# Separate readiness for three copies of V, a later gate broadcast, a one-bank gate through DRAM and new scheduler constants, in a two-branch attention kernel

## The chip, the cores and the metric

One core of a Trainium2 chip. The metric is device time in microseconds (us) of one execution. A kernel is run several times on a chip, alternating with the kernel before, and its median is given. A profiled execution gives a span from first to last instruction, some 2 us shorter than the measured time; spans are compared only with spans, times only with times.

Engines: PE is the matrix engine (PEld its weight loads), ACT the scalar engine, DVE the vector engine, POOL the GpSimd engine, SP the engine that issues most transfers.

## The reference, cut to what matters

```python
g = sigmoid((x * gate_w).sum(-1, keepdims=True))
a = softmax_attention(x, A_wqkv, A_wo)     # 2048 tokens, width 512, 32 heads of 16
b = linear_attention(x, B_wqkv, B_wo)      # phi = elu + 1
return g * a + (1 - g) * b
```

The softmax of `a` needs 32 x 2048 x 2048 exponentials. Cut into tiles of 128 keys by 512 queries that is 2048 score tiles, and they are nearly all of the kernel's work.

## The kernel before: the parts that matter

The kernel is built by a list scheduler written in the kernel itself. It holds tasks as generators, keeps a model of when each engine and each buffer is free, and each time emits the candidate that can start first. Some thirty constants steer its choices. The order on each engine is fixed when the program is built.

Score tiles leave PE in PSUM. Two thirds of them are read by ACT in pairs (one exponential of 128x1024 into a ring `P` of ten buffers), one third by DVE with an integer trick into `Z`. A `Z` tile stands for three terms, shifted by POOL or DVE; each term is multiplied in P.V with its own scaled copy of V. The three copies of a block of V are made so (the cast by DVE, two scalings by POOL):

```python
def t_v(t8, vb):
    ...                                   # V projection of one block into a bank
    yield dv(607, lambda: nc.vector.tensor_copy(Vc[:, 0, vs, :, :, 0:16], src), [r_bank[b]], [r_V[vs]])
    yield ("FREE", b)
    for k in range(1, NTERM):             # NTERM = 3
        yield po(690, lambda k=k: nc.gpsimd.tensor_scalar(... Vc[:, k, vs] <- Vc[:, 0, vs] * COEF[k] ...), [r_V[vs]], [r_V[vs]])
    yield ("FLAG", lambda: V_ready.add((t8, vb)))
...
def cand_pv():
    ...
    if (t8, w["kb"] // 4) not in V_ready:
        continue
```

One resource `r_V[vs]` and one flag stand for all three copies: a P.V that reads the plain copy waits for both scalings. The gate's logits come from 64 matmuls into four banks, after a broadcast of the gate weights on POOL:

```python
def t_gate():
    yield po(900, lambda: nc.gpsimd.tensor_copy(gwr, gwc... .to_broadcast([128, NCC, 128])), [r_gw], [r_gwr])
    ...
    for qc in range(NQC):                 # four banks, 16 matmuls of 32x512 each
        ...
        yield dv(607, lambda b=b: nc.vector.transpose(gl, bank(b)), ...)
        yield po(250, ...)
    yield ac(300, lambda: nc.scalar.activation(gt[:], ge[:], ACT.Exp, scale=-1.0), ...)
    ...
add_task(t_gate(), 0, 1, "GATE")
```

The softmax here doesn't subtract the row's maximum and nothing guards it: scores larger than these inputs give would overflow.

## Time and profile before

The time before is 675.63 us (median of 3 runs, 675.01 to 676.53). What matters of its profile (span 674.2 us):

| part of ACT's time | us |
|---|---|
| start to the first exponential | 9.31 |
| holes between exponentials up to 46 us (0.21, 2.48, 0.34, 0.17) | 3.20 |
| 695 exponentials of a pair of tiles, 0.917 each | 637.3 |
| other work of ACT between them (the rest) | 16.7 |
| last exponential ends at | 666.49 |
| drain from there to the end | 7.7 |

A hole is idle time of ACT; the drain is what follows the last exponential. From 46 us on ACT is idle only once more before its last exponential, for 0.11 us at 530.6. Most of the lines that carry this are in the prediction below. First, POOL's own timeline of the kernel before, around the largest hole (start, length, what, count, idle before it and what ended that):

```profile
22.38 0.61 POOL L1001 COPY T<-gwc 128x512 bf16<-128x512 bf16 x1 [1.23 <-DMA gwc<-in_gate_w_dram]
23.07 1.47 POOL L995 TENSOR_SCALAR Vc<-Vc 128x576 bf16<-128x576 bf16 x2
26.71 1.43 POOL L995 TENSOR_SCALAR Vc<-Vc 128x576 bf16<-128x576 bf16 x2 [2.17 <-DVE Vc L992]
```

The gate broadcast stands in POOL's queue ahead of the V scalings and waits 1.23 us for a transfer. Second, PE's instructions from the end of the last exponential to the end of the program (line, what, count, busy us, mean ns):

```profile
L383 PE MATMUL ps<-wA,OAT 128*32 128x512 bf16 x43 | 3.7, 381 | 0.1
L383 PE MATMUL ps<-wA,xnat 128*32 128x512 bf16 x32 | 2.7, 380 | 0.0
```

The drain is mainly 75 matmuls of the output projection that the scheduler had not placed earlier.

### The profile page before, as it was taken

To read this page: it belongs to the slowest core of one execution; us is meant where nothing else is said; L and a number is where in the kernel's file an instruction comes from. 1 tells how busy PE (TensorE), PEld (TensorE's weight loads), DVE (VectorE), ACT (ScalarE), POOL (GpSimd) and SP (SyncE) were. 2 spreads that over 40 slices of the span, in tenths; PEclk is the share of its full clock that TensorE was granted. 3 is DMA by queue.
4 is the path that set the end of the run, shared out by engine and by line. 5 is a ranking of instruction groups with operands and counts; after the bars stand their busy time and mean duration, and the time that the engine had idled before them with its cause. 6 is when DMAs were issued, how large, how long until landed. Compare 5 with 4: busy or idle time off the path is not lost.

```text
span 674.2 us, 23975 instructions
## 1 busy us (share of the span) xinstructions
PE 660.7 (98%) x9813; PEld 202.2 (30%) x9839; DVE 603.4 (89%) x1053; ACT 658.3 (98%) x735; POOL 559.4 (83%) x617
## 2 busy tenths in 40 slices
PE   8999999999999999999999999999999999999998
PEld 3322323232322232323333322232232332222222
DVE  6999989988888889989999888999899998899985
ACT  6899999999999999999999999999999999999996
POOL 3789888888978888888888888878888989887881
PEclk9999999999999999999999999999999999999999
DMA  6420001200000000000001000001010020000001
GB/s 133 135 84 11 6 1 36 70 10 2 3 10 1 10 2 3 10 2 11 4 2 45 30 10 1 8 12 30 6 34 10 18 42 25 24 19 11 26 17 33
DMA packets 28155, 15.96 MB, mean 24 GB/s; under 512 B 19984, under 2 KB 27024, under 8 KB 28048
## 3 DMA queue, kind: packets, MB, share of 16 engines
q1 hardware_dynamic: 26704, 13.92, 8.2%
q8 instruction: 79, 1.29, 0.8%
q10 hardware_dynamic: 1344, 0.52, 0.3%
q14 instruction: 28, 0.23, 0.1%
HBM read 6.69 MB, written 2.10 MB: 13 GB/s over the span
## 4 chain that ended last, share of the span: by engine, by line
PE 50%; ACT 31%; issue 12%; SPq 2%; DVE 2%; POOL 1%; DMA 1%; ACTq 0%; DVEq 0%; POOLq 0%
PE ps L377 39%; ACT P L778 30%; PE ps L383 10%; SPq L354 2%; DVE Z L692 1%; ACT eb L1083 1%; POOL Z L746 1%; DMA gwc<-in_gate_w_dram 1%; DVE Z L756 0%; POOL Vc L995 0%; SPq L358 0%; ACTq L1495 0%; DVE OAT L1059 0%; DVE wA L1176 0%; DVE T L1031 0%
## 5 line engine op out<-in xcount | busy, mean ns | idle before, releaser
L778 ACT ACTIVATE P<-ps 128x1024 bf16<-128x1024 f32 x695 | 645.5, 1117 | 3.9 <-PE ps L377 3.7
L746 POOL TENSOR_TENSOR Z<-Z,mcon 128x512 int32<-128x512 int32 x471 | 488.0, 1061 | 64.4 <-DVE Z L692 50.4
L692 DVE TENSOR_SCALAR Z<-ps 128x512 int16<-128x512 f32 x658 | 440.4, 683 | 57.2 <-PE ps L377 50.9
L377 PE MATMUL ps<-Qz,KT 32*128 32x512 bf16 x2048 | 271.8, 384 | 3.9 <-ACT P L778 1.7
L377 PE MATMUL ps<-Z,Vc 128*17 128x512 bf16 x1974 | 272.5, 382 | 0.5 <-DVE Z L756 0.3
L377 PE MATMUL ps<-P,Vc 128*17 128x512 bf16 x1390 | 245.0, 383 | 1.0 <-POOL Vc L995 1.0
L377 PEld LDWEIGHTS ps<-Qz,KT 32*128 32x128 bf16 x2048 | 67.8, 91 | 262.7 <-ACT P L778 228.7
L377 PEld LDWEIGHTS ps<-Z,Vc 128*17 128x17 bf16 x1974 | 60.9, 88 | 69.1 <-issue 44.2
L756 DVE TENSOR_SCALAR Z<-Z 128x1024 int16<-128x1024 int16 x187 | 77.3, 433 | 0.0
L377 PEld LDWEIGHTS ps<-P,Vc 128*17 128x17 bf16 x1390 | 55.5, 88 | 60.1 <-issue 46.0
L377 PE MATMUL ps<-warm 128*32 128x512 bf16 (+16 forms) x529 | 55.9, 326 | 4.7 <-issue 2.4
L383 PE MATMUL ps<-xT,wA 128*32 128x512 bf16 (+1 forms) x528 | 43.4, 376 | 0.0
L1084 POOL TENSOR_SCALAR eb<-eb 128x512 f32<-128x512 f32 x32 | 21.0, 656 | 18.7 <-DVE Z L756 10.1
L995 POOL TENSOR_SCALAR Vc<-Vc 128x576 bf16<-128x576 bf16 x32 | 21.7, 679 | 6.0 <-DVE Vc L992 2.3
L377 PEld LDWEIGHTS ps<-warm 128*32 128x32 bf16 (+1 forms) x555 | 19.4, 96 | 18.4 <-issue 10.3
L383 PE MATMUL ps<-wA,OAT 128*32 128x512 bf16 x256 | 23.0, 382 | 0.1
L1071 POOL TENSOR_TENSOR T<-T,rg 128x256 bf16<-128x256 f32 x31 | 19.6, 631 | 4.1 <-PE ps L377 1.0
L1083 ACT ACTIVATE eb<-ps 128x512 f32<-128x512 f32 x32 | 22.7, 709 | 0.0
L383 PE MATMUL ps<-xT,wB 128*32 128x512 bf16 x256 | 22.3, 382 | 0.0
L383 PE MATMUL ps<-wA,xnat 128*32 128x512 bf16 x256 | 22.3, 381 | 0.0
L1035 DVE STREAM_TRANSPOSE T<-ps 128x512 f32<-128x512 f32 x31 | 21.9, 706 | 0.1
L1085 DVE SCALAR_TENSOR_TENSOR phiK<-ps,eb 128x512 bf16<-128x512 f32 x32 | 21.7, 678 | 0.2 <-POOL eb L1084 0.2
(81 smaller groups left out, 276.1 us busy)
## 6 DMA issues: line engine op xcount, KB each, us to landing
Qz<-QT SPq DMA_DIRECT2D x120, 16.0 KB, 1.8
wA<-in_A_wqkv_dram SPq DMA_DIRECT2D x4, 384.0 KB, 4.3
wB<-in_B_wqkv_dram SPq DMA_DIRECT2D x4, 384.0 KB, 3.0
xnat<-in_A_x_dram SPq DMA_DIRECT2D x3, 512.0 KB, 3.8
out_dram<-outt SPq DMA_DIRECT2D x12, 128.0 KB, 1.7
wA<-in_A_wo_dram SPq DMA_DIRECT2D x1, 512.0 KB, 4.6
wA<-in_B_wo_dram SPq DMA_DIRECT2D x1, 512.0 KB, 6.5
out_dram<-wA SPq DMA_DIRECT2D x4, 128.0 KB, 1.7
```

Source lines behind the costliest of these rows:

```text
L377: return lambda: nc.tensor.matmul(o, lhsT=l, rhs=r, start=start, stop=stop, skip_group_check=sg)
L383: h = nc.tensor.matmul(o[32 * j:32 * j + 32], lhsT=l[:, 32 * j:32 * j + 32], rhs=r, start=start, stop=stop, skip_group_check=True)
L692: return C(DV, OPP, 533 * n + 74, lambda: nc.vector.tensor_scalar(o, i, ZB, 0.0, op0=ALU.add, op1=ALU.max), [r_bank[b] for b in bks], r_Z[ ...
L746: return C(PO, 400, 70 + 484 * n, lambda: nc.gpsimd.tensor_tensor(Z[:, z, 0:512 * n].bitcast(I32), Z[:, z0, 0:512 * n].bitcast(I32), mcon[ ...
L756: return C(DV, 450 if hot else 300, 69 + 134 * n, lambda: nc.vector.tensor_scalar(Z[:, z, 0:512 * n], Z[:, z0, 0:512 * n], float(m), None, ...
L778: return C(AC, 500, 427 * n + 49, lambda: nc.scalar.activation(P[:, slot, 0:512 * n], bank(b0, n), ACT.Exp, scale=ESC), [r_bank[b0 + k] fo ...
L995: yield po(690, lambda k=k: nc.gpsimd.tensor_scalar(Vc[:, k, vs].rearrange("p a b c -> p (a b c)"), Vc[:, 0, vs].rearrange("p a b c -> p ( ...
L1035: yield dv(607, lambda: nc.vector.transpose(T1[:, a, :], bank(7)), [r_bank[7]], [r_T1[a]])
L1071: yield po(640, lambda k=k: nc.gpsimd.tensor_tensor(dst_[:, k], src[:, k, :, 0:16], rgc[:, k].unsqueeze(2).to_broadcast([128, 16, 16]), AL ...
L1083: yield ac(480, lambda: nc.scalar.activation(eb[:, i, :], bank(b), ACT.Exp), [r_bank[b]], [r_eb[i]])
L1084: yield po(640, lambda: nc.gpsimd.tensor_scalar(eb[:, i, :], eb[:, i, :], 1.0 + 1e-6, 0.0, op0=ALU.min, op1=ALU.max), [r_eb[i]], [r_eb[i]])
L1085: yield dv(607, lambda: nc.vector.scalar_tensor_tensor(dst_ap, bank(b), 1e-6, eb[:, i, :], op0=ALU.max, op1=ALU.add), [r_bank[b], r_eb[i]] ...
```

## The change

Its intent: let P.V start on the plain copy of V as soon as that one is cast; keep the gate out of the way in the ramp; make the gate cheaper on PE, DVE and POOL, at the price of a trip through a small DRAM buffer; and search the scheduler's constants anew. The core of the diff:

```diff
-    HOT = 32.85
-    BACK = 980.186
-    SHB = 2
+    HOT = 31.272
+    BACK = 977.283
+    SHB = 3
 ... (thirteen more constants: PMIN, PLATE, SLK, DSL, AGE, PEP, HOLD, NACT, BIAS, TTOL, MTR, PQS, KR)
-        DMIN = 4
+        DMIN = 3
-        r_V = [R(f"V{p}") for p in range(NVQ)]
+        r_V = [[R(f"V{p}_{k}") for k in range(NTERM)] for p in range(NVQ)]
 ...
-        dma(SP, gwc[:], gate_w..., semG, 16, 3000.0, ...)
+        dma(SP, gwc[:], gate_w..., semG, 16, 6000.0, ...)
 ...
-                    if (t8, w["kb"] // 4) not in V_ready:
+                    if (t8, w["kb"] // 4, w["term"]) not in V_ready:
 ...
-                for x in (w["res"], r_V[vs]):
+                for x in (w["res"], r_V[vs][w["term"]]):
 ...
-            yield dv(607, ... [r_bank[b]], [r_V[vs]])
+            yield dv(607, ... [r_bank[b]], [r_V[vs][0]])
+            yield ("FLAG", lambda: V_ready.add((t8, vb, 0)))
 ...
-                                   ... [r_V[vs]], [r_V[vs]])
-            yield ("FLAG", lambda: V_ready.add((t8, vb)))
+                                   ... [r_V[vs][0]], [r_V[vs][k]])
+                yield ("FLAG", lambda k=k: V_ready.add((t8, vb, k)))
 
         def t_gate():
-            yield po(900, ... to_broadcast([128, NCC, 128])), [r_gw], [r_gwr])
+            yield po(400, ... to_broadcast([128, NCC, 32])), [r_gw], [r_gwr])
 ...          # one bank: 16 matmuls, four column groups side by side; one transpose
+            yield ac(230, ... ge[:, 0, :] <- exp(-logits, 128x16) ...)
 ...
+            yield ("DMA", scr, ge[:, 0, :], semGN, 16, ...)                     # rows to DRAM
+            for a in range(4):
+                yield ("DMA", gt[32 * a:32 * (a + 1), :, :], scr..., semGT, 64, ...)   # and back, spread
 ...
-        add_task(t_gate(), 0, 1, "GATE")
+        add_task(t_gate(), 0.5, 1.2, "GATE")
```

The number 6000.0 in the load of the gate weights is only the scheduler's belief of when that load lands; it makes the broadcast look ready later, and so it is emitted later.

More of the change, by code (lines that the diff above doesn't have):

```diff
@@ L159, in bass_gated_mix__mha_block__linear_attn_block__prompt_kernel @@
     FILL = 0.7
-    HOT = 32.85
-    BACK = 980.186
-    SHB = 2
+    HOT = 31.272
+    BACK = 977.283
+    SHB = 3
     why = [None]
-    PMIN = 2
-    PLATE = -199.667
-    SLK = 88.975
-    DSL = 843.776
+    PMIN = 1
+    PLATE = -168.321
+    SLK = 188.531
+    DSL = 812.862
     STICK = 65.578
@@ L171, in bass_gated_mix__mha_block__linear_attn_block__prompt_kernel @@
     DENS = 0.743
-    AGE = 300.0
-    PEP = 148.771
+    AGE = 140.993
+    PEP = 147.128
     PVD = 216
@@ L176, in bass_gated_mix__mha_block__linear_attn_block__prompt_kernel @@
     MZD = 0.0
-    HOLD = 109.508
-    NACT = 4
-    BIAS = 82.599
+    HOLD = 16.447
+    NACT = 5
+    BIAS = 65.881
     KEYW = 7.061
@@ L182, in bass_gated_mix__mha_block__linear_attn_block__prompt_kernel @@
     DTOL = 186.116
-    TTOL = 37.928
-    PKR, MTR, PQR, PQS, FR = 0.404, 8.73, 13.55, 1.600, 0.0
-    KR, KS, QR = 5.59, 1.48, 4.00
+    TTOL = 64.585
+    PKR, MTR, PQR, PQS, FR = 0.404, 8.00, 13.55, 1.667, 0.0
+    KR, KS, QR = 6.12, 1.48, 4.00
     NB = 2
@@ L231, in bass_gated_mix__mha_block__linear_attn_block__prompt_kernel @@
         T2 = SB([128, 2, 512], BF16, "T2")
-        gwr = T2[:, 0, :].rearrange("p (c n) -> p c n", c=NCC)
+        gwr = T2[:, 0, 0:128].rearrange("p (c n) -> p c n", c=NCC)
         OAT = SB([128, NT8, S], BF16, "OAT")
@@ L242, in bass_gated_mix__mha_block__linear_attn_block__prompt_kernel @@
         gt = SB([128, NQC, 16], FP32, "gt")
-        ge = SB([128, NQC, 16], FP32, "ge")
+        ge = SB([128, 2, 16], FP32, "ge")
+        gp = SB([128, 4, 16], FP32, "gp")
+        scr = nc.dram_tensor("gate_rows", [128, 16], FP32).ap()
         gnat = SB([128, NKB], FP32, "gnat")
@@ L288, in bass_gated_mix__mha_block__linear_attn_block__prompt_kernel @@
         r_mcon = R("mcon")
-        r_gt, r_ge, r_gl, r_gnat = R("gt"), R("ge"), R("gl"), R("gnat")
+        r_gt, r_ge, r_gl, r_gp, r_gnat, r_scr = R("gt"), R("ge"), R("gl"), R("gp"), R("gnat"), R("scr")
         r_OBT = [R(f"OBT{i}") for i in range(NKB)]
@@ L399, in bass_gated_mix__mha_block__linear_attn_block__prompt_kernel @@
         semGN = SEM("s_gn")
+        semGP = SEM("s_gp")
+        semGT = SEM("s_gt")
         semOB = [SEM(f"s_ob{i}") for i in range(2)]
@@ L418, in bass_gated_mix__mha_block__linear_attn_block__prompt_kernel @@
                 r_xT[t][h].tw = SP.free + 2900.0
-        dma(SP, gwc[:], gate_w.rearrange("(cc p) -> p cc", p=128), semG, 16, 3000.0, writes=[r_gw], noncontig=True, issue=500.0)
+        dma(SP, gwc[:], gate_w.rearrange("(cc p) -> p cc", p=128), semG, 16, 6000.0, writes=[r_gw], noncontig=True, issue=500.0)
         emit(DV, 200, lambda: nc.vector.memset(warm[:], 0.0), writes=[r_warm])
@@ L436, in bass_gated_mix__mha_block__linear_attn_block__prompt_kernel @@
         for p in range(NVQ):
-            emit(PO, 200, lambda p=p: nc.gpsimd.memset(Vc[:, 0, p].rearrange("p t h d -> p (t h) d")[:, :, 16:18], 1.0), writes=[r_V[p]])
+            emit(PO, 200, lambda p=p: nc.gpsimd.memset(Vc[:, 0, p].rearrange("p t h d -> p (t h) d")[:, :, 16:18], 1.0), writes=[r_V[p][0]])
         for k, m in enumerate(SHIFTS[1:]):
@@ L991, in t_v @@
             src = bank(b).rearrange("p (t h d) -> p t h d", t=4, h=8)
-            yield dv(607, lambda: nc.vector.tensor_copy(Vc[:, 0, vs, :, :, 0:16], src), [r_bank[b]], [r_V[vs]])
+            yield dv(607, lambda: nc.vector.tensor_copy(Vc[:, 0, vs, :, :, 0:16], src), [r_bank[b]], [r_V[vs][0]])
+            yield ("FLAG", lambda: V_ready.add((t8, vb, 0)))
             yield ("FREE", b)
@@ L996, in t_v @@
                                                                   Vc[:, 0, vs].rearrange("p a b c -> p (a b c)"), COEF[k], 1.0,
-                                                                  op0=ALU.mult, op1=ALU.mult), [r_V[vs]], [r_V[vs]])
-            yield ("FLAG", lambda: V_ready.add((t8, vb)))
+                                                                  op0=ALU.mult, op1=ALU.mult), [r_V[vs][0]], [r_V[vs][k]])
+                yield ("FLAG", lambda k=k: V_ready.add((t8, vb, k)))
@@ L1000, in t_gate @@
         def t_gate():
-            yield po(900, lambda: nc.gpsimd.tensor_copy(gwr, gwc[:].unsqueeze(2).to_broadcast([128, NCC, 128])), [r_gw], [r_gwr])
-            yield ("WAIT", lambda: ("x", 0) in flags and phi_free[0])
-            phi_free[0] = False
-            for qc in range(NQC):
-                b = yield ("BANK",)
-                for h in range(2):
-                    yield pe_step(2, 512, [mmt(bank(b), gwr[:, cc, :], xT[:, cc, 512 * qc:512 * (qc + 1)], start=(cc == 0), stop=(cc == NCC - 1))
-                                           for cc in (2 * h, 2 * h + 1)], [r_xT[qc][h], r_gwr], [r_bank[b]])
-                yield dv(607, lambda b=b: nc.vector.transpose(gl, bank(b)), [r_bank[b]], [r_gl, *r_outt])
-                yield ("FREE", b)
-                yield po(250, lambda qc=qc: nc.gpsimd.tensor_copy(ge[:, qc, :], gl.rearrange("p (a b) -> p a b", b=32)[:, :, 0]),
-                         [r_gl, *r_outt], [r_ge])
@@ L1013, in t_gate @@
-            phi_free[0] = True
-            yield ac(300, lambda: nc.scalar.activation(gt[:], ge[:], ACT.Exp, scale=-1.0), [r_ge], [r_gt])
-            yield po(200, lambda: nc.gpsimd.tensor_scalar(ge[:], gt[:], 1.0, None, op0=ALU.add), [r_gt], [r_ge])
-            yield dv(650, lambda: nc.vector.reciprocal(gt[:], ge[:]), [r_ge], [r_gt])
-            gp = ge[:].rearrange("p q c -> p (q c)")
-            yield po(200, lambda: nc.gpsimd.tensor_scalar(gp.rearrange("p (a u) -> p a u", a=4), gt[:].rearrange("p q (c a) -> p a (q c)", a=4),
-                                                          -1.0, 1.0, op0=ALU.mult, op1=ALU.add), [r_gt], [r_ge])
@@ L1020, in t_gate, with g4, go @@
-            for a in range(4):
-                yield ("DMA", gnat[32 * a:32 * (a + 1), :], gp[32 * a:32 * (a + 1), 16 * a:16 * (a + 1)], semGN, 64, 2500.0, [r_ge], [r_gnat], False, a == 0)
+            yield po(400, lambda: nc.gpsimd.tensor_copy(gwr, gwc[:].unsqueeze(2).to_broadcast([128, NCC, 32])), [r_gw], [r_gwr])
+            yield ("WAIT", lambda: all(("x", t) in flags for t in range(NQC)))
+            b = yield ("BANK",)
+            def g4(cc):
+                def go():
+                    for j in range(4):
+                        h = nc.tensor.matmul(bank(b)[32 * j:32 * j + 32], lhsT=gwr[:, cc, :], rhs=xT[:, cc, 512 * j:512 * (j + 1)],
+                                             start=(cc == 0), stop=(cc == NCC - 1), skip_group_check=True)
+                    return h
+                return go
@@ new lines, in t_gate @@
+            for h in range(2):
+                yield pe_step(2, 512, [g4(2 * h), g4(2 * h + 1)], [*[r_xT[t][h] for t in range(NQC)], r_gwr], [r_bank[b]])
+            yield dv(607, lambda: nc.vector.transpose(gl, bank(b)), [r_bank[b]], [r_gl, *r_outt])
+            yield ("FREE", b)
+            yield ac(230, lambda: nc.scalar.activation(ge[:, 0, :], gl.rearrange("p (a b) -> p a b", b=32)[:, :, 0], ACT.Exp, scale=-1.0),
+                     [r_gl, *r_outt], [r_ge])
+            yield po(150, lambda: nc.gpsimd.tensor_scalar(ge[:, 1, :], ge[:, 0, :], 1.0, None, op0=ALU.add), [r_ge], [r_ge])
@@ new lines, in t_gate @@
+            yield dv(170, lambda: nc.vector.reciprocal(ge[:, 0, :], ge[:, 1, :]), [r_ge], [r_ge])
+            yield ("DMA", scr, ge[:, 0, :], semGN, 16, 2500.0, [r_ge], [r_scr], False, True)
+            for a in range(4):
+                yield ("DMA", gt[32 * a:32 * (a + 1), :, :], scr.rearrange("(q i) b -> i q b", q=NQC), semGT, 64, 2800.0, [r_scr], [r_gt], False, a == 0)
+            yield po(200, lambda: nc.gpsimd.tensor_scalar(gp[:], gt[:].rearrange("p q (c a) -> p a (q c)", a=4), -1.0, 1.0, op0=ALU.mult, op1=ALU.add),
+                     [r_gt], [r_gp])
@@ L1022, in t_gate @@
+            for a in range(4):
+                yield ("DMA", gnat[32 * a:32 * (a + 1), :], gp[32 * a:32 * (a + 1), a, :], semGP, 64, 2500.0, [r_gp], [r_gnat], False, a == 0)
             yield ("FLAG", lambda: flags.add("gate"))
@@ L1101, in t_wo @@
         def t_wo():
-            yield ("WAIT", lambda: all((NT8 - 1, t) in K_ready and (NT8 - 1, t) in V_ready for t in range(NQC)))
+            yield ("WAIT", lambda: all((NT8 - 1, t) in K_ready and (NT8 - 1, t, NTERM - 1) in V_ready for t in range(NQC)))
             yield ("DMA", woA, A_wo.rearrange("(i p) n -> p i n", p=128), semWO, 32, 5000.0, [], [r_wAk], False, True)
```

## The prediction

> **What bounds the kernel now.** I read the page's part 1, then the table of stretches, then the timeline of each engine where ACT has holes. The attention has 4 x 16 x 32 = 2048 score tiles of 128x512. ACT takes 1390 of them (695 exponentials of two tiles each), DVE takes the other 658 with a bit trick (into Z), which POOL and DVE then shift twice each. All of them feed P.V on PE. Page and stretches (columns of a stretch: length, busy us and instructions of PE, PEld, DVE, ACT, POOL, then PE clock, DMA share, GB/s):
>
> ```profile
> PE 660.7 (98%) x9813; PEld 202.2 (30%) x9839; DVE 603.4 (89%) x1053; ACT 658.3 (98%) x735; POOL 559.4 (83%) x617
> ...
> 0.00:20.00 20.00, 18.05 (x268) 7.74 (x269) 14.28 (x26) 13.56 (x16) 9.44 (x32) 1.00 0.61 126
> 20.00:40.00 20.00, 18.86 (x377) 6.89 (x375) 17.97 (x31) 16.71 (x19) 16.02 (x20) 1.00 0.41 124
> 40.00:60.00 20.00, 20.00 (x264) 5.39 (x260) 18.91 (x35) 20.00 (x24) 16.62 (x22) 1.00 0.17 52
> 320.00:360.00 40.00, 39.77 (x816) 14.21 (x804) 36.98 (x67) 40.00 (x45) 34.32 (x37) 1.00 0.01 3
> ```
>
> From 40 us on ACT is busy in every microsecond until its last exponential; PE's 98% includes 529 warm-up matmuls that can give way. So the body is ACT's queue of work, and time can be won only before 40 us, after the last exponential, or by giving ACT less. ACT's own timeline (start, length, what, count, idle before it):
>
> ```profile
> 9.31 12.02 ACT L778 ACTIVATE P<-ps 128x1024 bf16<-128x1024 f32 x13 [0.54 <-PE ps L377]
> 21.54 1.02 ACT L778 ACTIVATE P<-ps 128x1024 bf16<-128x1024 f32 x1 [0.21 <-PE ps L377]
> 25.05 9.46 ACT L778 ACTIVATE P<-ps 128x1024 bf16<-128x1024 f32 x10 [2.48 <-PE ps L377]
> 34.85 2.86 ACT L778 ACTIVATE P<-ps 128x1024 bf16<-128x1024 f32 x3 [0.34 <-PE ps L377]
> 37.88 7.44 ACT L778 ACTIVATE P<-ps 128x1024 bf16<-128x1024 f32 x8 [0.17 <-PE ps L377]
> ...
> 201.59 158.87 ACT L778 ACTIVATE P<-ps 128x1024 bf16<-128x1024 f32 x173
> ...
> 649.79 16.70 ACT L778 ACTIVATE P<-ps 128x1024 bf16<-128x1024 f32 x18
> ```
>
> One exponential costs (158.87 - 1.11) / 172 = 0.917 us of ACT (1.11 is the group's mean length; neighbours overlap). After the ramp's first there are holes of 0.21 + 2.48 + 0.34 + 0.17 = 3.20 us. The last exponential ends at 649.79 + 16.70 = 666.49, and the drain to 674.2 is 7.7 us. What holds the 2.48 us open is seen in DVE, POOL and PE there, and in the chain of waits (its pieces: start, length, what):
>
> ```profile
> 18.28 4.05 DMA gwc<-in_gate_w_dram
> 22.33 0.05 issue
> 22.38 0.61 POOL T L1001
> ...
> 20.77 0.68 DVE L992 CAST Vc<-ps 128x512 bf16<-128x512 f32 x1
> ...
> 23.07 1.47 POOL L995 TENSOR_SCALAR Vc<-Vc 128x576 bf16<-128x576 bf16 x2
> ...
> 22.72 0.39 PE L377 MATMUL ps<-Qz,KT 32*128 32x512 bf16 x2
> 23.27 0.35 PE L377 MATMUL ps<-warm 128*128 128x448 bf16 x1 [0.16 <-issue]
> 24.60 0.40 PE L377 MATMUL ps<-P,Vc 128*17 128x512 bf16 x4 [0.98 <-POOL Vc L995]
> ```
>
> V's second block is cast by 21.45. POOL could scale its two copies at once, but its queue holds the gate broadcast first, and that waits for the gate weights, the last small load behind a serial run of transposing loads. The copies end at 24.54; P.V waits for both although it reads the unscaled one; the ten P buffers are full, so the fifteenth exponential waits for the P.V that frees the fifth buffer, 24.60 + 0.40 = 25.00.
>
> **The Trainium skill.** "Trainium Architecture — The Big Picture", section "Inside one NeuronCore", says that each engine has its own instruction stream and meets the others only through semaphores. The trace agrees: an idle POOL instruction (1.23 us of waiting) delays PE and ACT by queue order. "ScalarE: Activation LUTs", section "What ACT_TABLE_LOAD costs", gives 186 ns + 0.833 ns per element, with 93 ns overlapped; so halving the 1024 elements saves 427 ns. The trace has 0.917 us per exponential against an estimate of 0.946 by that formula, and the 512-wide exponential eb at 56.26 is followed at 56.73, 0.47 us later: the difference, 0.45, agrees. "TensorEngine Tiling (Array Packing)", section "Available Configurations", lists four tiles of 128x32; the trace agrees, 16 such projection matmuls take 1.05 us at 21.74, some 0.21 per wave of four after the first. "DMA: Bandwidth & Descriptors", section "Two DMAs through the same engine are not ordered", asks for the semaphore between a write and a dependent read; the changed program waits so between the gate rows' write and their reads, a full landing more. Small ones took 1.7 (gnat) to 4.0 us (gwc).
>
> **The change, part by part.** The order of the changed program was built, not run.
> 1. Own readiness per V copy. In the changed order PE runs the same two score matmuls at about 22.7, then at once the P.V of the unscaled second block, with no wait on POOL. So it starts at 22.7 + 0.32 = 23.0 instead of 24.60, ends about 23.4, and the fifteenth exponential starts at 23.4 instead of 25.05. The one before has a single P.V wave ahead of it instead of two, 0.21 less, so the hole of 0.21 goes. The hole left is 23.4 - (21.33 + 1.02) = 1.05. Sum here: (0.21 + 2.48) - 1.05 = **1.64 us** won.
> 2. Gate broadcast later. POOL now does two shifts, the second block's copies and another shift first (20.0 + 2 x 1.06 + 1.5 + 1.06, estimate 24.6), when the gate weights (22.33) have long landed: POOL's 1.23 us of waiting goes. But PE no longer waits there, so it adds nothing to part 1.
> 3. One bank of gate logits. 64 matmuls of 32x512 become 16: 12 waves x 0.21 = 2.5 us of PE, three transposes x 0.71 = 2.1 us of DVE, about 0.8 + 0.4 of POOL (four copies x 0.20 go, a 128-column broadcast instead of 512), and on ACT the 128x64 exponential (its neighbours start 0.14 apart) becomes 128x16, saving under 0.1. All but ACT's part lies beside ACT's queue. Before 40 us freed PE time may shorten the 0.34 and 0.17 holes; by hand I find one P.V-bound hole of about 0.25 at the gate matmuls, so **0.2 us** for the pair.
> 4. The trip through DRAM. One write and four reads before the gate can be used. My estimate: logits ready near 34, write issued near 38 behind eight Qz copies, landed 40, reads issued over 2.4 us (four gnat issues took 2.41) and landed near 45. The first reader is POOL near 47, and the first use of the gate is at 58.6 today. Hidden, with 2 us to spare on POOL: **0**.
> 5. Retuned scheduler constants. DVE takes 659 tiles, ACT 694 pairs and one single: 0.917 - 0.47 = **0.45 us** less on ACT. POOL gets 473 shifts instead of 471 (+2.1 us) and DVE one tile more (0.68), on engines with 83 and 89%: free. In the drain the last wait on DVE is followed by 8 output matmuls instead of 12, **0.2 us**.
> Sum: 1.64 + 0.2 + 0.05 + 0.45 + 0.2 = 2.5 us off 675.63 gives 673.1.
>
> **Rivals.** (a) *The hole is hidden anyway*: if ACT were paced by PE or DVE later, a ramp gain would be eaten by a later wait. For it: PE is 98% busy, DVE 89%. Against: no hole on ACT after 38 us; then 675. (b) *The DRAM trip becomes the new wait*: POOL stands in order behind the read of gt; if the landing takes 4 us each as gwc did, twice, POOL would stall 2 to 3 us, shifts come late, and PE's P.V with them. The ten P buffers hide most; it would give back 1 to 2 us: 674 to 675. (c) *The retuned schedule removes more*: 0.917 us per exponential may hold small waits that never show as idle because neighbours overlap; if the new constants remove a fifth of a possible 10 us, 671. (d) *ACT's new bound in the ramp is the P ring once more*: the 1.05 stays or grows if V's third and fourth blocks come late; then 674.
>
> **Range and chances.** The centre is 673.1; (b) and (d) pull up by one or two, (c) down by two; runs differ by 0.75 around the median. 80%: 671.4 to 674.9. Two per cent is 13.5 us, more than all holes and the drain's spare together (3.7 + part of 7.7), so faster is very unlikely. Slower by 13.5 would take a schedule that starves ACT, and the instruction order shows the same interleave: 1%.
>
> **What would show it.** In the changed profile: the P.V by the second V block starts near 23.0 with no wait on POOL's copies; the hole on ACT near 22.4 is about 1 us; the broadcast on POOL is 128 wide, after the second block's copies, and waits for nothing; the last exponential ends near 664.2, ahead of 666.49; drain near 7.5; no wait on the gate's reads over 1 us. The prediction is wrong if ACT shows new holes after 40 us, if the cadence in the long row moves off 0.917 by more than 0.004 (2.8 us over 694), or if the drain grows.

## The result

The changed kernel took 674.41 us (674.00 to 674.79, 4 runs) beside 675.77 us of the kernel before on the same chip (675.01 to 676.53, 4 runs). The ratio is 0.998, with a 95% interval of 0.9962 to 0.9997. (A ratio here and below is the mean of one kernel's runs over the mean of the other's of the same rounds, so not quite the ratio of the medians.) That is within 2%, 1.4 us lower, and inside the predicted range; the profiled span went from 674.2 to 672.6. A second set of runs gave 673.79 beside 676.01 (ratio 0.9964), 2.2 us lower. The prediction's sum was 2.5.

ACT's timeline of the changed kernel, from the first exponential on:

```profile
9.11 13.17 ACT L782 ACTIVATE P<-ps 128x1024 bf16<-128x1024 f32 x14 [0.53 <-PE ps L379]
23.25 4.69 ACT L782 ACTIVATE P<-ps 128x1024 bf16<-128x1024 f32 x5 [0.97 <-PE ps L379]
28.71 5.08 ACT L782 ACTIVATE P<-ps 128x1024 bf16<-128x1024 f32 x5 [0.77 <-PE ps L379]
34.03 1.02 ACT L782 ACTIVATE P<-ps 128x1024 bf16<-128x1024 f32 x1 [0.23 <-PE ps L379]
34.95 0.22 ACT L1021 ACTIVATE ge<-outt 128x16 f32<-128x16 f32 x1
35.06 21.23 ACT L782 ACTIVATE P<-ps 128x1024 bf16<-128x1024 f32 x23
...
653.98 10.73 ACT L782 ACTIVATE P<-ps 128x1024 bf16<-128x1024 f32 x12
```

Before the fifteenth exponential 0.21 + 2.48 has become 0.97. But there is a hole of 0.77 at 28.71 that nobody asked for. The last exponential ends at 653.98 + 10.73 = 664.71, so the drain is 7.9. POOL and PE around the first hole, of the changed kernel:

```profile
21.52 1.42 POOL L1000 TENSOR_SCALAR Vc<-Vc 128x576 bf16<-128x576 bf16 x2
24.41 0.42 POOL L1006 COPY T<-gwc 128x128 bf16<-128x128 bf16 x1 [0.35 <-DVE Z L760]
...
46.41 0.30 POOL L1028 TENSOR_SCALAR gp<-gt 128x64 f32<-128x64 f32 x1
57.29 0.25 POOL L1079 TENSOR_TENSOR rg<-rec,gt 128x32 f32<-128x32 f32 x1
```

```profile
22.48 0.39 PE L379 MATMUL ps<-Qz,KT 32*128 32x512 bf16 x2
22.80 0.60 PE L379 MATMUL ps<-P,Vc 128*17 128x512 bf16 x5
...
26.53 0.46 PE L385 MATMUL ps<-wA,xT 128*32 128x128 bf16 x19
27.94 0.40 PE L385 MATMUL ps<-wA,xT 128*32 128x128 bf16 x13 [0.96 <-issue]
```

Three readings. P.V starts at 22.80 and waits for nothing; in the kernel before it started at 24.60. The scalings now end at 22.94, ahead of the broadcast. And in the middle of the third V projection PE does nothing for 0.96 us while waiting for no semaphore ("issue"): this is what opens the 0.77 hole. In the trace PE's instructions arrive as blocks of 16384 bytes by a queue of their own, in the page's list of queues (packets, MB, share):

```profile
q8 instruction: 78, 1.28, 0.8%
```

PE dispatches about 250 matmuls and weight loads to each of these blocks (20070 to 78 blocks here). The third block's fetch started at 25.46 and took 0.96 us; from PE's last instruction before the stall, at 26.77, to the next 1.18 us passed. PE had dispatched 380 instructions since the fetch before, where 250 are usual: the fetch began late. PE ran out of instructions (what speaks for this is under e5 to e8); 78 fetches of this kind pass in this profile, and this was the only one that PE was seen to wait for. (Fetches and dispatched instructions, here and below, are counted from the packed trace; no view shows them.)

The difference of the two profiled spans, in parts: start 0.20 earlier, holes 3.20 to 1.97 (1.23 less), the rest of the time between first and last exponential 0.35 less (666.49 - 9.31 - 3.20 = 653.98 against 664.71 - 9.11 - 1.97 = 653.63; the single tile in place of a pair was to bring 0.45), drain 0.2 longer. Together 1.6.

### The profile page after: what moved, and what is told of

Same layout as the page of the kernel before. It is cut to its first block, busy times and chain, and to the rows that moved or that the text cites. A ratio compares the mean times of both kernels' runs of the same rounds, so it can differ in the third digit from the quotient of the medians.

```text
span 672.6 us, 23844 instructions
## 1 busy us (share of the span) xinstructions
PE 662.4 (98%) x9743; PEld 200.1 (30%) x9743; DVE 600.1 (89%) x1051; ACT 657.8 (98%) x735; POOL 562.4 (84%) x615
## 3 DMA queue, kind: packets, MB, share of 16 engines
HBM read 6.72 MB, written 2.11 MB: 13 GB/s over the span
## 4 chain that ended last, share of the span: by engine, by line
PE 63%; ACT 27%; issue 9%; DVE 1%; ACTq 0%
PE ps L379 49%; ACT P L782 26%; PE ps L385 14%; ACT eb L1093 1%; PE ps L1013 0%; PE ps L910 0%; DVE OAT L1069 0%; ACTq L1505 0%; DVE T L1041 0%; DVE T L1066 0%; ACT wA L1239 0%; DVE rec L1064 0%; ACT KT L934 0%; DVE rg L1065 0%; DVE warm L425 0%
## 5 line engine op out<-in xcount | busy, mean ns | idle before, releaser
L379 PE MATMUL ps<-Z,Vc 128*17 128x512 bf16 x1977 | 279.4, 382 | 0.0
L379 PE MATMUL ps<-P,Vc 128*17 128x512 bf16 x1389 | 248.6, 383 | 0.0
L379 PEld LDWEIGHTS ps<-Z,Vc 128*17 128x17 bf16 x1977 | 62.7, 88 | 75.3 <-issue 49.1
L760 DVE TENSOR_SCALAR Z<-Z 128x1024 int16<-128x1024 int16 (+1 forms) x187 | 78.4, 435 | 0.2
L379 PE MATMUL ps<-warm 128*32 128x512 bf16 (+17 forms) x505 | 61.7, 336 | 1.2 <-DVE dummy L431 1.2
L385 PE MATMUL ps<-wA,xT 128*32 128x128 bf16 x1024 | 21.9, 220 | 1.0 <-issue 1.0
L385 PE MATMUL ps<-phiK,xnat 128*32 128x512 bf16 x256 | 22.6, 382 | 0.0
```

Of the source, the lines that this page charges most:

```text
L379: return lambda: nc.tensor.matmul(o, lhsT=l, rhs=r, start=start, stop=stop, skip_group_check=sg)
L385: h = nc.tensor.matmul(o[32 * j:32 * j + 32], lhsT=l[:, 32 * j:32 * j + 32], rhs=r, start=start, stop=stop, skip_group_check=True)
L760: return C(DV, 450 if hot else 300, 69 + 134 * n, lambda: nc.vector.tensor_scalar(Z[:, z, 0:512 * n], Z[:, z0, 0:512 * n], float(m), None, ...
```

## The experiments

**Theories.** (A) The prediction's: P.V's wait for the scaled copies is what held the hole, and readiness for each copy removes it, 1.64 us; the moved broadcast adds nothing. (B) The order of POOL's queue is what matters: once the scalings stand ahead of the broadcast, the shared wait costs nothing. (C) The constants are worth one half exponential and 0.2 us of drain. (D) They are worth much more, since they fit the schedule to the code.

For each profiled run the same ledger was made; "body" is the time from first to last exponential less the holes, and the last column counts output-projection matmuls after the last exponential. The number of exponentials counts a single tile as half.

| run | exponentials | start | holes to 46 us | body | drain | matmuls left |
|---|---|---|---|---|---|---|
| kernel before | 695 | 9.31 | 3.20 | 653.98 | 7.67 | 75 |
| changed kernel | 694.5 | 9.11 | 1.97 | 653.63 | 7.87 | 73 |
| changed, again (e5) | 694.5 | 9.77 | 1.20 | 653.20 | 7.86 | 74 |
| own readiness alone (e1) | 695 | 8.87 | 3.59 | 654.24 | 8.99 | 105 |
| late broadcast alone (e2) | 694 | 8.59 | 3.96 | 653.11 | 11.27 | 149 |
| changed, shared wait (e3) | 694.5 | 9.10 | 2.50 | 653.81 | 7.86 | as changed |
| new constants alone (e4) | 695 | 9.23 | 1.50 | 655.41 | 10.44 | 132 |
| changed, retuned (e9) | 691.5 | 8.64 | 2.28 | 650.81 | 8.09 | 80 |
| the same, shared readiness (e10) | 693 | 9.17 | 2.28 | 651.75 | 7.72 | 79 |
| before, retuned (e11) | 693.5 | 9.12 | 6.33 | 652.31 | 7.94 | 74 |
| changed, old constants (e12) | 696 | 9.20 | 4.09 | 654.97 | 10.75 | 140 |

The body follows the number of exponentials to within about 0.4 us (but for e4's, which has a hole of 0.99 in it); the drain follows the matmuls left: (11.27 - 7.67) / (149 - 75) = 0.049 us each, against 0.054 from the trace of e2, where groups of 16 such matmuls start 0.86 to 0.87 apart.

### e1: own readiness alone

The kernel before with only the `r_V` and `V_ready` lines of the diff.

> The kernel before with its constants and gate, and only the own readiness of the three V copies. In its built order the P.V of V's second block stands right after the two score matmuls at 22.7 us with no wait on POOL, and POOL's gate broadcast has moved behind the block's copies by itself. Theory (own readiness closes the hole by letting the scheduler issue P.V early): the hole on ACT before the fifteenth exponential falls from 2.48 to about 1.0 us, as in the changed kernel. Rival (the late broadcast is what matters): with the gate weights' model latency left as it was, the hole stays near 2.5. Second point: if the 0.96 us wait of PE for nothing visible at 27 us in the changed kernel comes from PE running earlier than its instructions arrive, it must show here too, 0.5 to 1.2 us within the third V projection, and the gain is about 0.8 us instead of 1.5. Still 695 exponentials of full width.

Measured: 677.26 us beside 676.06, ratio 1.0016 (1.0001 to 1.0031). ACT's timeline:

```profile
23.15 4.69 ACT L778 ACTIVATE P<-ps 128x1024 bf16<-128x1024 f32 x5 [0.94 <-PE ps L377]
28.85 6.00 ACT L778 ACTIVATE P<-ps 128x1024 bf16<-128x1024 f32 x6 [1.01 <-PE ps L377]
```

and POOL's:

```profile
21.34 1.42 POOL L996 TENSOR_SCALAR Vc<-Vc 128x576 bf16<-128x576 bf16 x2
22.94 0.61 POOL L1002 COPY T<-gwc 128x512 bf16<-128x512 bf16 x1 [0.18 <-DMA gwc<-in_gate_w_dram]
```

The hole closed as expected, yet the kernel became slightly slower. Note POOL: the broadcast's code was not touched, and it moved behind the scalings by itself. So this run closes the hole but cannot tell A from B. The time went into the drain (30 more matmuls of the output projection, 1.3 us), a hole of 1.48 at 36.33 behind a run of P.V matmuls, and the stall on instructions again (1.01 at 28.85).

### e2: late broadcast alone

```diff
-        dma(SP, gwc[:], gate_w..., semG, 16, 3000.0, ...)
+        dma(SP, gwc[:], gate_w..., semG, 16, 6000.0, ...)
-        add_task(t_gate(), 0, 1, "GATE")
+        add_task(t_gate(), 0.5, 1.2, "GATE")
```

> The kernel before with only the gate broadcast made later (model latency of the gate weights 6000, release 0.5). POOL's broadcast stands behind the second block's copies, so those end near 23.0 instead of 24.54. But in the built order P.V of that block stands behind the third block's projection, which waits for the K copy (23.5) and takes 0.9 us. Theory: the hole is hardly closed, 2.0 to 2.4 us instead of 2.48, and PE waits for nothing at POOL. Rival (the POOL wait was the whole cause): the hole falls to about 1.1. ACT has 694 exponentials instead of 695 here, worth 0.9 us by itself, so the time is no measure; the hole is.

Measured: 678.84 us, ratio 1.0039 (1.0022 to 1.0055). PE's timeline shows why the hole stayed at 2.37 though POOL had done the scalings by 23.73 (22.31 + 1.42), 0.84 us before P.V:

```profile
23.67 1.08 PE L383 MATMUL ps<-wA,xT 128*32 128x128 bf16 x64
24.57 0.59 PE L377 MATMUL ps<-P,Vc 128*17 128x512 bf16 x5
```

The scheduler put the whole third V projection ahead of the P.V that frees a `P` buffer. The right order on POOL is not enough when PE's order is unlucky. Here 149 output matmuls were left for the drain.

### e3: the changed kernel with the shared wait put back

The order of all instructions is kept; only each P.V is made to wait for all three copies.

```diff
+        for at, blocks in pv_log:
+            for bl in blocks:
+                PE.ops[at][0].append((PO.sem, PO.cover(v_copy[(*bl, NTERM - 1)].idx)))
```

> The changed kernel in the same order, every instruction the same, but each P.V made to wait for all three copies of its V block again. Theory (the order was worth the time, not the wait): POOL's copies of the second block end at 22.94, so P.V starts at 23.0 instead of 22.80, the hole grows from 0.97 to 1.1 to 1.25 us, the later blocks have their copies long before; the time is the changed kernel's, +0.0 to +0.3 us. Rival (the dependency itself is worth the 1.5 us): the hole goes back toward 2.5 us and the time up by 1 us or more.

Measured: 674.13 us, ratio 0.9974 (0.9959 to 0.9988), no slower than the changed kernel (674.41). It was run at another time. The hole was 1.46 in this profile, above the expected 1.1 to 1.25. PE and POOL:

```profile
23.31 0.39 PE L379 MATMUL ps<-Qz,KT 32*128 32x512 bf16 x2
23.63 0.60 PE L379 MATMUL ps<-P,Vc 128*17 128x512 bf16 x5
```

```profile
21.76 1.42 POOL L1002 TENSOR_SCALAR Vc<-Vc 128x576 bf16<-128x576 bf16 x2 [0.32 <-DVE Vc L998]
```

P.V starts 0.32 us after the two score matmuls, as in the changed kernel (22.48 and 22.80), and the scalings end at 23.18, before it: the wait that was put back held nothing up. What was later is the projection ahead of them: PE stood idle for 0.45 until 22.34, which the profile puts down to DVE; an `xT` load landed at 22.20 as well, against 21.20 in the changed kernel. The wait that part 1 of the change removes costs nothing measurable once the order is that of the changed kernel. That speaks for B.

### e4: the new constants alone

The kernel before, with only the constants of the diff.

> The kernel before with only the retuned scheduler constants. In its built order P.V of the second block stands right behind the two score matmuls but waits for POOL's second copy (shared readiness), and POOL has the broadcast behind the copies. Theory: hole of about 1.1 to 1.3 us, so the constants alone would have closed most of it; the PE wait near 27 us shows too (0.4 to 1.0). 695 full exponentials, so no 0.45 us there. Rival (own readiness needed): hole 2 us or more.

Measured: 678.50 us, ratio 1.0035 (1.0020 to 1.0050). POOL and ACT:

```profile
21.65 1.43 POOL L995 TENSOR_SCALAR Vc<-Vc 128x576 bf16<-128x576 bf16 x2
23.14 0.61 POOL L1001 COPY T<-gwc 128x512 bf16<-128x512 bf16 x1
```

```profile
23.58 9.89 ACT L778 ACTIVATE P<-ps 128x1024 bf16<-128x1024 f32 x10 [0.95 <-PE ps L377]
```

With shared readiness and the broadcast released as early as before, the constants happened to put the scalings first, and the hole was 0.95. So the hole closes without part 1 and without part 2. Theory A is out as the only way; B holds in every profile so far, with e2's caveat. And the constants on the old code cost 2.4 us, by a drain of 10.4 and a hole of 0.99 us on ACT at 367.3.

### e5 to e8: is the instruction stall part of the kernel?

e5 is the changed kernel again. e6 has more, smaller warm-up matmuls at its start, so that the edges of the instruction blocks fall elsewhere. e7 holds the four bulk weight loads back until PE is past the stall's place, order kept. e8 does both.

```diff
 # e6
-        emit(PE, 3000, [mm(bank(...), warm[:, 0:128], warm[:]) for b in range(8)], ...
+        emit(PE, 3000, [mm(bank(...), warm[:, 0:128], warm[:]) for b in (0, 1, 2, 7)]
+             + [mm(ps[..., 3584:3600], warm[:, 0:32], warm[:, 0:16], sg=True) for i in range(68)], ...
 # e7
+        for op in SP.ops:
+            if op[3] is semWA:
+                op[0].append((PE.sem, 85))
```

> The changed kernel once more, for comparison on this chip. If the late instruction fetch near 25.5 us belongs to the kernel and is no chance of one profile, TensorE stalls again for 0.8 to 1.2 us near 27 us and ScalarE has a hole of 0.6 to 0.9 us near 28.7 us; if it was chance, no stall over 0.5 us there. Time 674 to 675.

> The changed kernel with 60 to 64 more small warm-up matmuls at its start, so that the points at which TensorE runs out of one block of fetched instructions fall elsewhere in the program; results unchanged. Theory that the stall comes from the place of the block's edge within the dense third projection of V: the stall of 1 us at 27 us goes or moves away from it, and the hole of 0.77 at 28.7 falls below 0.3. Theory that the bulk loads of weights crowd out any fetch in 24 to 27 us: a stall near 0.9 us stays, at some other place before 28 us. Time 673.7 to 674.6.

> The changed kernel, same order of instructions, with the four bulk loads of weights (384 KB each, issued from 20.1 us) held back until TensorE is past the third projection of V (near 28 us). Theory that the loads crowd out the instruction fetch: the third fetch comes in time, the stall of 1 us at 27 us is below 0.4, the hole of 0.77 goes below 0.3, time lower by 0.5 to 0.7 us than the changed kernel. Theory that the fetch is late by its own latency: stall and hole stay as they are, 0.8 to 1.2 and 0.6 to 0.9. Risk: what needs the weights first waits instead, a hole over 0.5 us between 30 and 40 us.

> Both edits together. If only the loads matter: as the run with the loads held back. If only the block's edge matters: as the run with more small matmuls. If each takes part of it: no stall over 0.3 us before 30 us and a hole below 0.2 near 28.7; time 673.4 to 674.2.

Measured, beside 676.01 of the kernel before: e5 673.79 (ratio 0.9964), e6 673.98 (0.9967), e7 673.47 (0.9960), e8 674.20 (0.9967). None had the stall, not even e5, the unchanged program. Its ACT timeline:

```profile
9.77 13.17 ACT L782 ACTIVATE P<-ps 128x1024 bf16<-128x1024 f32 x14 [0.53 <-PE ps L379]
23.91 9.36 ACT L782 ACTIVATE P<-ps 128x1024 bf16<-128x1024 f32 x10 [0.97 <-PE ps L379]
33.50 1.02 ACT L782 ACTIVATE P<-ps 128x1024 bf16<-128x1024 f32 x1 [0.23 <-PE ps L379]
```

So my expectation that the stall belongs to the program fell: the same program has it in one execution and not in another, and with no stall in the control, the three edits can show nothing about its cause by the time. What can be said from all fourteen profiles: the stall near 27 us is there when the third fetch starts after PE has dispatched 850 or more instructions (e4: 850, a short gap of 0.43; changed kernel: 852, 1.18; e3: 857, 1.10; e2: 864, 1.07; e1: 888, 1.37; e9: 890, 1.40; e12: 916, 1.74), and absent when it starts by 831 (kernel before 814, e5 804, e10 831). In all seven PE stops after 960 or 961 instructions and goes on 2.27 to 2.48 us after the start of that fetch; in the other seven profiles it comes to this point 2.54 us or more after the start, and doesn't stop. So PE did wait for the block; why the block is asked for later in one execution than in another is what is not known. With the loads held back, e7 fetched at 705. This hints that the bulk loads make the fetch late, but one profile each is no proof, and the cause of the late fetch stays open.

### e9 to e12: code and constants apart

The three single-part runs (e1, e2, e4) all gave their win back in the drain or in holes, which leaves the question what the code is worth when each variant has constants that fit it. So the constants of three variants were searched again, equally long (some 2100 random steps, judged by the finishing time that the scheduler's own model computes while building). Two constants of that model itself, SWITCH and FILL, were left alone. e9 is the changed kernel; e10 is the changed kernel with shared readiness; e11 is the kernel before. e12 is the changed kernel with the old constants, no search.

```diff
 # e9, some of the constants against the changed kernel
-    HOT = 31.272
-    BACK = 977.283
-    DSL = 812.862
+    HOT = 74.986
+    BACK = 2083.400
+    DSL = 2590.600
 # e10, ahead of its own search: one resource and one flag for the three copies
-        r_V = [[R(f"V{p}_{k}") for k in range(NTERM)] for p in range(NVQ)]
+        r_V = [R(f"V{p}") for p in range(NVQ)]
```

> The changed kernel's code with the scheduler's constants searched again (some 2100 random steps, judged by the finishing time that the scheduler itself computes while it builds the program; that figure was 660.1 for the kernel before, 658.7 for the changed one, 656.1 here). Theory that the length of the drain and the small holes, hence the constants, carry as much as the parts of the change: about 2.5 us below the changed kernel, 671 to 672, drain below 7.5 us. Rival, that the scheduler's figure is fitted and the chip doesn't follow: 673.5 to 675, as the changed kernel.

> The changed kernel with the readiness of its V copies shared again (the first part undone) and its constants searched as long as in the run before (the scheduler's own figure 657.9). Theory that own readiness is worth its hole, 1.2 to 1.6 us, at equal tuning: 672.6 to 674, that is 1.2 to 2.2 above the run with own readiness and equal tuning, and a hole of about 2.4 us before the 15th exponential. Rival, that a search finds a schedule without that hole by other means: hole below 1.2 and time within 0.5 us of the run with own readiness.

> The kernel before, none of the change's parts, with only its constants searched as long (the scheduler's own figure 658.8 against 660.1). If the change's gain is retuning alone: as low as the changed kernel with the same search, 671 to 672. If its parts are worth what the prediction summed (2.5 us less the half exponential): 674 to 675, 2 to 3 us above the changed kernel with the same search.

> The changed kernel with all constants of the kernel before put back (retuning undone, the other parts kept; the scheduler's own figure 663.6). Theory that the constants fit the code they were searched with: 4 to 5.5 us slower than the changed kernel, 678 to 679.5, from the drain (10 us or more) while the hole at the 15th exponential stays near 1.0. Rival, that the constants were worth only the half exponential and 0.2 us of drain, as predicted: 674.3 to 675.2.

Measured, beside 676.09 of the kernel before (11 runs; the others 6 runs each):

| run | median us | ratio to the kernel before (95%) |
|---|---|---|
| e9, changed, retuned | 671.58 | 0.9927 (0.9915 to 0.9939) |
| e10, the same with shared readiness | 672.62 | 0.9947 (0.9935 to 0.9959) |
| e11, before, retuned | 674.95 | 0.9983 (0.9967 to 1.0000) |
| e12, changed, old constants | 679.58 | 1.0047 (1.0030 to 1.0064) |

**e9** beats both kernels, by 4.5 us and some 2 to 3. The page's group of DVE's bit trick shows how, first the changed kernel, then e9:

```profile
L696 DVE TENSOR_SCALAR Z<-ps 128x512 int16<-128x512 f32 x659 | 440.2, 682 | 56.7 <-PE ps L379 51.1
```

```profile
L696 DVE TENSOR_SCALAR Z<-ps 128x512 int16<-128x512 f32 x665 | 444.1, 682 | 52.3 <-PE ps L379 45.7
```

Six tiles moved from ACT to DVE, three exponentials of a pair, 3 x 0.917 = 2.75 us off the engine that bounds the body. The drain, which I had expected below 7.5, was 8.09, and this profile had the instruction stall, too (0.99).

**e10** is 1.04 us above e9 by the medians, 1.35 by the ratios (0.0020 of 676). Its time is at the lower edge of what theory A expected (672.6 to 674; 1.2 to 2.2 above e9), its hole is not: 0.21 + 1.62 instead of 2.4, and not below the rival's 1.2 either. All its holes sum to the same 2.28 as e9's. ACT, then POOL:

```profile
21.41 1.02 ACT L782 ACTIVATE P<-ps 128x1024 bf16<-128x1024 f32 x1 [0.21 <-PE ps L379]
24.05 9.48 ACT L782 ACTIVATE P<-ps 128x1024 bf16<-128x1024 f32 x10 [1.62 <-PE ps L379]
```

```profile
21.60 1.43 POOL L999 TENSOR_SCALAR Vc<-Vc 128x576 bf16<-128x576 bf16 x2
24.49 0.42 POOL L1005 COPY T<-gwc 128x128 bf16<-128x128 bf16 x1 [0.35 <-DVE Z L760]
```

The scalings are again ahead of the broadcast and end at 23.03, before the P.V that reads them (23.60). Of the 1.62 some 0.63 was a wait of PE for a transfer of `xT`. What separates e10 from e9 is the body: 1.5 exponentials more, 1.4 us. Whether separate readiness gave the search that freedom or luck did, one search each cannot tell.

**e11** is shown by its slowest execution: the profiled one took 677.52 us, the other five 674.43 to 675.14. POOL and ACT:

```profile
23.59 0.89 POOL L1001 COPY T<-gwc 128x512 bf16<-128x512 bf16 x1 [2.63 <-DMA gwc<-in_gate_w_dram]
24.57 1.52 POOL L995 TENSOR_SCALAR Vc<-Vc 128x576 bf16<-128x576 bf16 x2
```

```profile
26.81 1.02 ACT L778 ACTIVATE P<-ps 128x1024 bf16<-128x1024 f32 x1 [4.43 <-PE ps L377]
```

The broadcast is still ahead of the scalings; the gate weights came 1.2 us later than in the profile of the kernel before, POOL waited 2.63, and the hole grew to 4.43. PE stood idle for 2.71 us behind the same wait, and its clock was lowered meanwhile (columns as for e12 below):

```profile
25.00:26.00 1.00, 0.00 (x0) 0.00 (x0) 1.00 (x2) 0.00 (x0) 0.92 (x2) 0.78 1.02 409
26.00:27.00 1.00, 0.85 (x24) 0.59 (x28) 0.37 (x1) 0.19 (x1) 0.09 (x1) 0.50 0.07 28
```

In this execution the holes (6.33) cost more than the 1.5 exponentials won. How large they were in the other five is not known; the gain by the medians is 1.1 us. It ends 3.4 us above e9 with the same search, which speaks against retuning alone as the gain, with one search for each.

**e12** refutes theory C. With the old constants the changed code is 5 to 6 us slower than with the new ones (679.58 against 673.79 and 674.41), though its first hole is closed. ACT and PE of this profile:

```profile
23.35 4.69 ACT L782 ACTIVATE P<-ps 128x1024 bf16<-128x1024 f32 x5 [0.97 <-PE ps L379]
29.62 1.02 ACT L782 ACTIVATE P<-ps 128x1024 bf16<-128x1024 f32 x1 [1.59 <-PE ps L379]
31.56 1.02 ACT L782 ACTIVATE P<-ps 128x1024 bf16<-128x1024 f32 x1 [0.91 <-PE ps L379]
```

```profile
L385 PE MATMUL ps<-wA,OAT 128*32 128x512 bf16 x76 | 5.9, 380 | 0.0
L385 PE MATMUL ps<-wA,xnat 128*32 128x512 bf16 x64 | 4.9, 379 | 0.0
```

The lower pair is PE after the last exponential: 140 output matmuls left instead of 73, 2.9 us of drain. Another 1.5 exponentials are 1.4 us. These two belong to the schedule and make 4.3 of it. The holes of 1.59 and 0.91 belong to this execution (680.85 us; the four of its six runs with a mean clock of 0.999 or 1.000 took 678.68 to 679.61): PE stalled on instructions for 1.52 us, and then its clock was lowered. Stretches of one microsecond from 28 us (length, busy us and instructions of PE, PEld, DVE, ACT, POOL, then the PE clock, the DMA share and GB/s):

```profile
28.00:29.00 1.00, 0.40 (x16) 0.26 (x16) 0.00 (x0) 0.04 (x1) 0.55 (x1) 0.92 0.03 12
29.00:30.00 1.00, 1.00 (x12) 0.29 (x15) 0.93 (x2) 0.38 (x1) 0.15 (x1) 0.50 0.00 0
...
33.00:36.00 3.00, 3.00 (x48) 0.85 (x40) 2.27 (x4) 2.77 (x3) 2.92 (x4) 1.00 0.02 5
```

## Why the prediction was right, and where its reasons were not

The time was inside the range. By its own steps:

- **Part 1, the hole: size right, cause wrong.** P.V was to start at 23.0, it did at 22.80; the hole was to be 1.05, it was 0.97; 0.21 + 2.48 - 0.97 = 1.72 won against 1.64. The size came right because it was read from the built order, which holds all parts of the change at once; such a reading cannot tell which part made the order. The prediction gave all of it to own readiness. With the shared wait put back in the same order the time stayed (e3), and two programs with shared readiness have the scalings first and a smaller hole than before (e4 0.95, e10 1.62). What the three have in common is the order: the scalings ahead of the broadcast on POOL, and P.V ahead of the third projection on PE. In the changed order the shared wait could have cost 0.14 us at most (scalings done at 22.94, P.V at 22.80).
- **Part 2 is the step that failed**: "PE no longer waits there, so it adds nothing to part 1". This splits what cannot be split: the 1.64 us were put down to the wait that is gone, and the runs show that they belong to the order. The broadcast behind the scalings is enough to close most of the hole, provided PE's order doesn't put the projection ahead of P.V (e2). And where it stays in front, the hole depends on when a transfer happens to land: 2.48 in the kernel before, 4.43 in e11. Part 1 alone (e1) and the constants alone (e4) each lead the scheduler to the whole order, part 2 alone (e2) to POOL's half of it, so their worths don't add.
- **Part 3**: the pair 0.34 + 0.17 became one hole of 0.23, next to the gate's matmuls, where the prediction put 0.25; 0.28 won against 0.25 with the 0.05 for ACT. That the cheaper gate won it is not shown: e4, with the old gate, has a single hole of 0.23 there too (at 33.70), and e12, with the new gate, has three (0.22, 0.17, 0.23). No run took part 3 or 4 alone.
- **Part 4, the DRAM trip, was right.** The write was issued at 37.69 (predicted 38) and took 4.3 us to land where some 2 were predicted; the reads were issued from 42.05 and had landed by 45.06 (predicted 45), POOL used them at 46.41 (predicted 47) without waiting, and the first use of the gate was at 57.29. Rival (b) did not come about, with 1.35 us to spare. The margin was not tested by an experiment.
- **Part 5, the constants.** The half exponential was there (the body is 0.35 shorter for the predicted 0.45); the drain grew by 0.2 instead of shrinking by 0.2. But the term was mis-sized as a description of what the constants do: without them the same code is 5 to 6 us slower (e12), and on the old code they cost 2.4 (e4).
- **Sum**, as measured in the profiles: 1.72 + 0.28 + 0.35 - 0.2 = 2.15 against 2.5, and the second set of runs measured 2.2 by the medians. The first measured 1.4; its profiled execution had 0.77 lost to the stall on instruction fetch, which was in neither the prediction nor its rivals. (With the start 0.20 earlier and this 0.77 one is back at the 1.6 between the spans.) That the stall also explains the times of the unprofiled runs of that set is possible, but it was not shown.

Three signs of a wrong prediction were named. New holes after 40 us did not occur in the changed kernel. The cadence stayed: (181.76 - 1.11) / 197 = 0.917 us in its longest row of exponentials (198 from 195.00 on). The drain grew, by 0.2. When parts of the change were taken alone it grew by 1.3 to 3.6 us, and e4 had a new hole at 367.3.

## What to carry to other kernels

When a list scheduler lays out the program, judge a change by the order that it produces, and first look at what stands ahead in an in-order queue: a small task that waits for a transfer delays everything behind it, and moving it can be worth as much as removing a dependency. Taking parts of such a change alone measures each part plus a schedule that no longer fits, so give every variant an equal search of its constants before comparing, and more than one search if the difference is small. And keep a ledger of start, holes, number of operations on the bounding engine, and drain for each profile: here it showed where the time of each profiled execution went, where the total alone would have misled.

## What the Trainium skill lacked or had wrong

- "Runtime: NRT & Kernel Launch", section "Instruction fetch mechanics": it holds that fetching blocks of 16 KiB (256 instructions) is mostly hidden because engines dispatch slower than the fetch fills. In six of fourteen profiles the third fetch of PE's instructions began late, and 1.07 to 1.74 us passed between two of its instructions near 27 us, in a dense run of 128x128 matmuls; in a seventh (e4) it was 0.43. In the other seven the longest gap from 24 to 31 us is 0.31, in e11 0.45. The same program has the stall in one execution and not in another. The trace fits that section's two lines of 16 KiB, not its 128 KiB for PE: in the changed kernel PE ran dry some 490 instructions after the start of the second fetch (from 472 dispatched to 961), with 250 to a block.
- "TensorE: Matmul & The Clock Gate", section "Part 1: The HAM clock gate (the "warmup" mystery)": it gives an idle window of about 3.4 us before the clock is halved. In e12 a stall of 1.52 us was followed by a halved clock: the granted clock was 0.50 from 28.84 to 32.25 us, and 128x512 matmuls took 0.60 to 0.62 us instead of 0.38. In e11, with PE idle for 2.71 us from 23.44 on, it was 0.50 from 25.55 to 28.96, so it fell 2.11 us into the idle time. After stalls of 0.96 us (changed kernel) and 1.18 us (e9) the clock stayed at 1.00 and such matmuls at 0.38 to 0.39 us. Where between these the limit lies, and whether the length of the stall alone decides, was not measured.
